# Weight conversion's sign word by GpSimd's rounding addition in place of VectorE's mask, and w_out's row 7 used as a split pair in chunk 0's first half

## The chip, the cores and the metric

The kernel runs on one core of a Trainium2 chip. The metric is device time in microseconds (us), as the median of three runs. The engines are PE (TensorE: matmuls), DVE (VectorE), ACT (ScalarE), POOL (GpSimd) and SP (SyncE, which here only issues DMAs).

## The reference, cut to what matters

```python
B, H, S, Ns, D = (8, 8, 512, 32, 64)      # x: B,H,S,D   state: B,H,Ns,D
scores = scale * np.matmul(x, state.transpose(0, 1, 3, 2))
a = softmax(scores);  xread = np.matmul(a, state)
scores2 = scale * np.matmul(state, x.transpose(0, 1, 3, 2))
a2 = softmax(scores2);  sread = np.matmul(a2, x)
attn_out = np.concatenate([xread, sread], axis=2)
x = attn_out.transpose(0, 2, 1, 3).reshape(B * S, H * D)     # rows: x's and the state's
h = x @ w_in;  g = h - np.tanh(h);  out = g @ w_out           # 512 -> 2048 -> 512
```

`softmax` stands here for the five lines that subtract the maximum, exponentiate, and divide by the sum. `w_in` (512 x 2048) and `w_out` (2048 x 512) arrive as 64-bit floats, so each value is two 32-bit words in memory, and the kernel makes 32-bit floats of them itself.

## The kernel before, in words

The work is cut into chunks: chunk i holds the 512 x-rows of batch i, and a last chunk the rows of the state reads. For a chunk, `hidden(f)` makes one of 16 slices of 128 hidden columns by matmuls into PSUM (`hps`), `finish` makes `t = tanh` on ACT and `g = hps - t` on DVE, and `output(f)` adds g times row f of w_out (128 x 512) into four PSUM banks (`ops`). Since w_in enters only behind the attention, the first chunks multiply the state by w_in once (`mps`, copied to `mr` by ACT) and use that product as the hidden layer's weights.

Most products are made of pairs: a number is split into a high part (ACT's CAST to fp32r) and a rest (DVE's subtraction), both at line 106, and three matmuls (lines 575, 576, 577, or 515, 516, 517) replace one of full precision. In the first half of chunk 0, rows listed in `PLAIN` are not split: one matmul in plain fp32 (line 573) does it, which the profile shows as two records. The attention weights of chunk 1 (`aT`) are ready when DVE has made their low part, and chunk 1's first hidden matmuls wait for them. The program does eight rows of chunk 0, then all of chunk 1, then the rest of chunk 0.

`Weight.load` brings a 128 x 512 block of 64-bit words by SP into one of six buffers (`w10d`, `wo3d` and the like: `w10` is a block of w_in, `wo3` row 3 of w_out). `Weight.steps` makes it 32-bit in four instructions: DVE shifts the high word (line 138), DVE masks the sign bits into a 16-bit field of a helper tile (line 139, `w10r`), ACT writes the low word's rest into the other field (line 140), and DVE adds the two (line 141). The helper tiles, the unsplit rows of w_out (`wor`) and some others share four buffers (tag `c2`). There are 32 such blocks.

Each engine runs its instructions in a fixed order. The start follows the string `SEQ`; behind it a scheduler sets each engine's order when the program is built, from dependences, from `issue_after` gates and from its own estimate of times. `CONV` and `WO` say at which step a block is converted, `SPLITS` at which step a plain row is split for later use.

Of the kernel before, what the change touches and what calls it, by code (L numbers as in the profile page):

```python
# [13 lines left out]
U16 = mybir.dt.uint16  # L14
ALU = mybir.AluOpType
# [15 lines left out]
EARLY_S = 2  # L31
LONE = 1
HALT = 8
PLAIN = (0, 1, 7)
TURN = ((0, 1, 2, 3), (1, 0, 3, 2))


# [1 line left out]
def attention_ffn(ctx: ExitStack, tc: tile.TileContext, xT, xn, bd, bh, sp, sm, sl, win, wout, xout, tout, sout):  # L39
# [10 lines left out]
    nc = tc.nc  # L50
# [57 lines left out]
    class Weight:  # L108
# [17 lines left out]
        def steps(self, dst):  # L126

            if self.src.dtype == F32:
                return [lambda: None] * 3 + [lambda: nc.gpsimd.tensor_copy(dst, self.raw)]
            low, high = self.raw[:, :, 0], self.raw[:, :, 1]  # L130
            u, i = dst.bitcast(U32), dst.bitcast(I32)


            r = pool.tile([P, 512, 2], U16, tag="c2", name=f"{self.name}r", bufs=CSB)
            rest, top = r[:, :, 0], r[:, :, 1]
            return [

                lambda: nc.vector.tensor_scalar(u, high, 3, 0x3FFFFFFF, ALU.logical_shift_left, ALU.bitwise_and),
                lambda: nc.vector.tensor_single_scalar(top, self.raw.bitcast(U16)[:, :, 3], 0xC000, ALU.bitwise_and),
                lambda: nc.scalar.activation(rest, low, AF.Copy, scale=2.0**-29),  # L140
                lambda: nc.vector.tensor_add(i, i, r.rearrange("p f w -> p (f w)").bitcast(I32)),
            ]

        def convert(self, dst):
            return [step() for step in self.steps(dst)][1].ins


    m_first = {}
# [147 lines left out]
    def convert_wout(f, part):  # L296
        if f in PLAIN:
            if f // 2 not in plain:
                plain[f // 2] = big(f"wp{f}", [P, 2, DM], F32)
            return part.convert(plain[f // 2][:, f % 2])  # L300
        w = pool.tile([P, 512], F32, tag="c2", name=f"wor{f}", bufs=CSB)
        made = part.convert(w)
        wo[f] = big(f"wo{f}", [P, 2, DM], F32R)
        low = split(wo[f][:, 0], wo[f][:, 1], w)[1].ins
        return low if f in (2, 3) else made
# [3 lines left out]
    def split_row(f):  # L309
        wo[f] = big(f"wo{f}", [P, 2, DM], F32R)  # L310
        split(wo[f][:, 0], wo[f][:, 1], plain[f // 2][:, f % 2])
# [179 lines left out]
    class Chunk:  # L491
# [31 lines left out]
        def finish(self, f, ps):  # L523
            i, n = self.i, self.n
            t = pool.tile([P, 512], F32, tag="t", name=f"t{i}_{f}", bufs=TB)[:, :n]
            if CL <= i < B:
# [4 lines left out]
                return  # L531
            if i == 0 and f in PLAIN:
                g = self.g[f] = pool.tile([P, 512], F32, tag="g", name=f"g{i}_{f}", bufs=GB)
# [33 lines left out]
        def add(self, f, t):  # L567
            g, o = self.g[f], self.o[t]
            tok = slice(t * P, t * P + P)
            stop = f + 1 in self.begins or f == NFF - 1 or (self.i == B and t == 1 and f == NFF - 3)  # L570
            if self.i == 0 and f in PLAIN:
                w = plain[f // 2][:, f % 2]
# [78 lines left out]

    CONV = [1, 1, 8, 8, 9, 10, 11, 12, 13, 14]
    WO = [0, 2, 3, 4, 5, 6, 9, 10, 11, 12, 13, 14, 15, 16]
    SPLITS = [8,9,10]
    split_it = iter(PLAIN)
    PAIRS = [1, 1, 9, 9, 11, 11, 13, 13, 15, 15]
    rest = w0[1][2:] + w0[2] + w0[3]
# [237 lines left out]
    for st, (i, f) in enumerate(order):  # L895
# [34 lines left out]
            with ExitStack() as gates:  # L930
                for x in tanhs[max(st - 1, 0)]:
                    gates.enter_context(tc.issue_after(x))
                if st in (HALT, HALT + 1):
                    gates.enter_context(tc.issue_after(settled[1]))
                for _ in range(SPLITS.count(st)):
                    split_row(next(split_it))
# [276 lines left out]
```

## Time and profile before

| what | us |
|---|---|
| median of 3 runs | 637.64 |
| lowest, highest run | 637.53, 640.27 |
| span of the profiled execution | 635.4 |
| PE busy in it | 627.7 |
| DVE busy in it | 474.8 |
| ACT busy in it | 380.3 |
| POOL busy in it | 24.0 |

The span goes from the first to the last instruction. The profiled execution's own time is its span and what lies around it; against the median of the runs that is 637.64 - 635.4 = 2.2 us, and a span is turned into a time by adding them. The granted PE clock is 1.000 of full speed over the whole span.

### The profile page before, as it was taken

The numbers are of one execution on the slowest core, as the hardware profiler recorded it, in microseconds if no ns is written. First come the engines' busy times: TensorE is split into PE (matmuls) and PEld (weight loads), VectorE is DVE, ScalarE is ACT, GpSimd is POOL, SyncE is SP. The second block draws the span as 40 slices with busy tenths as digits, with TensorE's granted clock in tenths as the row PEclk, the third lists the DMA queues.
The fourth block names the chain that finished last, engine by engine and source line by source line (L and its number), as shares of the span: only waits on it lengthen the run. The fifth ranks groups of instructions, "written<-read, shape, count | busy, mean of one in ns | idle before, by whom it ended". The sixth has DMA issues, their size and how long they took to land.

```text
span 635.4 us, 9664 instructions
## 1 busy us (share of the span) xinstructions
PE 627.7 (99%) x3490; PEld 489.2 (77%) x3490; DVE 474.8 (75%) x770; ACT 380.3 (60%) x656; POOL 24.0 (4%) x38
## 2 busy tenths in 40 slices
PE   7999999999999999999999999999999999999997
PEld 4456677777777788778888788788888888888996
DVE  5999997686667956999445889989955789754542
ACT  5777777567666757676554675637565554533432
POOL 0000000000000000000000000000000001233200
PEclk9999999999999999999999999999999999999999
DMA  9993866568879856679952644765555537999700
GB/s 319 361 387 132 297 226 183 187 190 254 261 239 294 271 198 219 217 268 346 364 189 87 206 144 141 230 226 163 169 178 181 172 100 239 299 338 329 252 1 33
DMA packets 67439, 141.21 MB, mean 222 GB/s; under 512 B 6976, under 2 KB 28736, under 8 KB 67392
## 3 DMA queue, kind: packets, MB, share of 16 engines
q1 hardware_dynamic: 64544, 131.95, 63.4%
q0 software_dynamic: 2560, 8.39, 4.0%
q8 instruction: 27, 0.44, 0.3%
q10 hardware_dynamic: 288, 0.26, 0.1%
q14 instruction: 20, 0.16, 0.1%
HBM read 96.01 MB, written 44.56 MB: 221 GB/s over the span
## 4 chain that ended last, share of the span: by engine, by line
PE 94%; DVE 3%; ACT 2%; DMA 1%; issue 0%; ACTq 0%
PE X L1048 14%; PE hps L515 10%; PE hps L516 10%; PE hps L517 10%; PE ops L575 10%; PE ops L576 9%; PE ops L577 9%; PE Y0m L1048 5%; PE Y1m L1048 5%; PE mps L242 2%; PE mls L249 2%; PE ops L573 2%; PE rps L461 1%; PE pps L440 1%; PE hps L789 1%; PE mps L187 1%
## 5 line engine op out<-in xcount | busy, mean ns | idle before, releaser
L575 PE MATMUL ops<-wo,g 128*128 128x512 f32 x244 | 96.2, 400 | 0.0
L576 PE MATMUL ops<-wo,g 128*128 128x512 f32 x244 | 95.5, 391 | 0.0
L515 PE MATMUL hps<-aT,m 128*128 128x512 f32 x240 | 94.4, 395 | 0.0
L516 PE MATMUL hps<-aT,m 128*128 128x512 f32 x240 | 93.8, 391 | 0.1
L517 PE MATMUL hps<-aT,m 128*128 128x512 f32 x240 | 93.4, 390 | 0.0
L577 PE MATMUL ops<-wo,g 128*128 128x512 f32 x244 | 88.4, 396 | 0.0
L536 DVE TENSOR_TENSOR t<-hps,t 128x512 f32<-128x512 f32 (+1 forms) x77 | 48.7, 633 | 45.2 <-ACT t L536 44.8
L530 ACT ACTIVATE t<-hps 128x512 f32<-128x512 f32 x64 | 38.4, 599 | 66.3 <-PE hps L517 66.0
L536 ACT ACTIVATE t<-hps 128x512 f32<-128x512 f32 (+1 forms) x77 | 42.5, 552 | 56.7 <-PE hps L517 56.1
L530 DVE TENSOR_TENSOR G<-hps,t 128x512 f32<-128x512 f32 x64 | 43.9, 687 | 28.9 <-ACT t L530 28.7
L106 DVE TENSOR_TENSOR g<-t,g 128x512 fp32r<-128x512 f32 (+1 forms) x77 | 48.5, 632 | 16.1 <-ACT g L106 15.2
L575 PEld LDWEIGHTS ops<-wo,g 128*128 128x128 f32 x244 | 45.6, 188 | 17.4 <-ACT t L536 2.3
L106 ACT CAST g<-t 128x512 fp32r<-128x512 f32 (+1 forms) x77 | 44.3, 576 | 23.2 <-DVE t L536 22.8
L577 PEld LDWEIGHTS ops<-wo,g 128*128 128x128 f32 x244 | 45.5, 188 | 12.6 <-issue 2.5
L515 PEld LDWEIGHTS hps<-aT,m 128*128 128x128 f32 x240 | 45.1, 188 | 12.4 <-issue 2.0
L576 PEld LDWEIGHTS ops<-wo,g 128*128 128x128 f32 x244 | 45.8, 188 | 10.5 <-issue 1.1
L516 PEld LDWEIGHTS hps<-aT,m 128*128 128x128 f32 x240 | 45.1, 188 | 9.9 <-DVE aT L106 0.5
L517 PEld LDWEIGHTS hps<-aT,m 128*128 128x128 f32 x240 | 45.0, 188 | 9.4
L1048 PE MATMUL X<-g0m,W0m 128*128 128x512 f32 x192 | 47.8, 389 | 0.0
L1048 PE MATMUL X<-g1m,W1m 128*128 128x512 f32 x192 | 45.8, 389 | 0.0
L106 ACT CAST g1m<-G 128x1024 fp32r<-128x1024 f32 x28 | 29.2, 1054 | 27.0 <-PE X L1048 9.9
L1086 POOL DMA_DIRECT2D wl<-wod x32 | 23.3, 728 | 574.2 <-DMA wn<-wf 526.6
(275 smaller groups left out, 1134.5 us busy)
## 6 DMA issues: line engine op xcount, KB each, us to landing
mr<-md SPq DMA_DIRECT2D x26, 512.0 KB, 4.3
xT<-in_xT SPq DMA_DIRECT2D x16, 512.0 KB, 6.1
md<-st SPq DMA_DIRECT2D x64, 128.0 KB, 3.1
xn<-in_xn SPq DMA_DIRECT2D x16, 512.0 KB, 5.6
wsd<-ws SPq DMA_DIRECT2D x16, 512.0 KB, 4.7
wod<-wo SPq DMA_DIRECT2D x32, 256.0 KB, 7.3
W0m<-wsd SPq DMA_DIRECT2D x16, 512.0 KB, 3.6
W1m<-wsd SPq DMA_DIRECT2D x16, 512.0 KB, 4.7
```

What stands on the lines that cost most here:

```text
L106: return nc.scalar.copy(hi, src), (sub or nc.vector).tensor_sub(lo, src, hi)
L242: made = nc.tensor.matmul(pss[e], s0[rows, x, 2 * p + e], t[rows, y], start=(n == 0), stop=(n == 2))
L515: nc.tensor.matmul(ps, mhi[k][:, cols], ahi[:, k], start=(k == 0), stop=False)
L516: nc.tensor.matmul(ps, mhi[k][:, cols], alo[:, k], start=False, stop=False)
L517: made = nc.tensor.matmul(ps, mlo[k][:, cols], ahi[:, k], start=False, stop=(k == nk - 1))
L530: main(nc.scalar.activation(t, ps, AF.Tanh), nc.vector.tensor_sub(g, ps, t))
L536: tanhs.append((nc.scalar.activation(t, ps, AF.Tanh).ins, nc.vector.tensor_sub(t, ps, t).ins))
L575: nc.tensor.matmul(o, g[:, 0, tok], w[:, 0], start=(f in self.begins), stop=False)
L576: nc.tensor.matmul(o, g[:, 0, tok], w[:, 1], start=False, stop=False)
L577: return nc.tensor.matmul(o, g[:, 1, tok], w[:, 0], start=False, stop=stop).ins
L1048: made = nc.tensor.matmul(out[t], w[:, e, x, cols], y[:, e], start=first and j == 0 and e == 0 and c == 0, stop=last and j == 3 and e == 1 ...
L1086: nc.gpsimd.dma_start(wo[f][:, :, cols].bitcast(F32), wod[:, f % 2, half, f // 2])
```

## The change

The mask on DVE goes. GpSimd reads the topmost 16 bits of each 64-bit word as a number, adds 1.5 * 2^37 and subtracts it again in 32-bit floats, which rounds to a multiple of 2^14, and writes that into the helper tile's field. The shift on DVE no longer masks. Row 7 leaves `PLAIN`, so it is split when it is converted, its g is split too, and the later split of row 7 goes.

```diff
-PLAIN = (0, 1, 7)
+PLAIN = (0, 1)
+COARSE = 1.5 * 2.0**37
...
-                lambda: nc.vector.tensor_scalar(u, high, 3, 0x3FFFFFFF, ALU.logical_shift_left, ALU.bitwise_and),
-                lambda: nc.vector.tensor_single_scalar(top, self.raw.bitcast(U16)[:, :, 3], 0xC000, ALU.bitwise_and),
+                lambda: nc.vector.tensor_single_scalar(u, high, 3, ALU.logical_shift_left),
+                lambda: nc.gpsimd.tensor_scalar(top, self.raw.bitcast(U16)[:, :, 3], COARSE, COARSE, ALU.add, ALU.subtract),
...
-            return [step() for step in self.steps(dst)][1].ins
+            return [step() for step in self.steps(dst)][0].ins
...
-    SPLITS = [8,9,10]
+    SPLITS = [8,9]
```

The scheduler then sets other orders. In the changed kernel every line behind line 33 has a number one higher. On ACT, in the start, the order before was as follows; `mr` and `at` are what the hidden matmuls of chunk 0's first four slices read, and `w11r` is the helper tile of a block of w_in.

```order
L784 COPY mr_136<-mps_237 64x2x128 x2
L140 ACTIVATE w10r<-w10d 128x512
L784 COPY mr_136<-mps_255 64x2x128 x2
L742 COPY at_275<-aps_267 128x512
L784 COPY mr_187<-mps_237 64x2x128 x2
L784 COPY mr_187<-mps_255 64x2x128 x2
L792 ACTIVATE t_0_287<-hps_0_253 128x512
L792 ACTIVATE t_1_290<-hps_1_251 128x512
L140 ACTIVATE w11r<-w11d 128x512
```

At the same place the changed kernel has this order on ACT.

```order
L785 COPY mr_136<-mps_237 64x2x128 x2
L141 ACTIVATE w10r<-w10d 128x512
L141 ACTIVATE w11r<-w11d 128x512
L785 COPY mr_136<-mps_255 64x2x128 x2
L743 COPY at_275<-aps_267 128x512
L785 COPY mr_187<-mps_237 64x2x128 x2
```

The helper `w11r` has moved ahead of the two copies from `mps_255` and of the copy `at_275`.

Further on, ACT splits row 3 of w_out (`wo_410`). `mps_322` and `mps_323` are the first pair of state-times-w_in products there, `mps_388` and `mps_389` the second pair. Before:

```order
L140 ACTIVATE wo3r<-wo3d 128x512
L207 COPY mr_312<-mps_322 128x512
L106 CAST m_561<-mr_187 128x1024
L207 COPY mr_313<-mps_323 128x512
L106 CAST wo_410<-wor_404 128x512
L140 ACTIVATE wo4r<-wo4d 128x512
L140 ACTIVATE wo5r<-wo5d 128x512
L207 COPY mr_312<-mps_388 128x512
L106 CAST wo_467<-wor_461 128x512
```

The same place on ACT in the changed kernel:

```order
L208 COPY mr_312<-mps_322 128x512
L107 CAST m_563<-mr_187 128x1024
L141 ACTIVATE wo3r<-wo3d 128x512
L208 COPY mr_313<-mps_323 128x512
L208 COPY mr_312<-mps_388 128x512
L208 COPY mr_313<-mps_389 128x512
L107 CAST wo_410<-wor_404 128x512
L537 ACTIVATE t_4_418<-hps_4_415 128x512
```

Row 3's CAST has moved behind both copies of the second pair.

On DVE the subtraction that needs this CAST stood here before, with rows 4 and 5 of w_out behind it.

```order
L141 ISA wor_404<-wor_404,wo3r 128x1024
L106 TENSOR_TENSOR m_561<-mr_187,m_561 128x1024
L106 TENSOR_TENSOR wo_410<-wor_404,wo_410 128x512
L138 TENSOR_SCALAR wor_461<-wo4d 128x512
L139 TENSOR_SCALAR wo4r<-wo4d 128x512
L138 TENSOR_SCALAR wor_502<-wo5d 128x512
```

In the changed kernel the same place on DVE reads as follows.

```order
L142 ISA w_366<-w_366,w13r 128x1024
L142 ISA wor_404<-wor_404,wo3r 128x1024
L107 TENSOR_TENSOR wo_410<-wor_404,wo_410 128x512
L139 TENSOR_SCALAR wor_461<-wo4d 128x512
L139 TENSOR_SCALAR wor_502<-wo5d 128x512
L537 TENSOR_TENSOR t_4_418<-hps_4_415,t_4_418 128x512
```

The masks are gone, and `wo_410` follows at once on the addition of row 3. From here to the first low part of `aT` the changed kernel's DVE list holds what the list before held, without the masks of rows 4 to 7, and with two more subtractions: row 7 of w_out (which stood behind `aT` before) and its g.

## Rows read from the trace of the kernel before

**Rows 1.** The page: span, and busy time, share and instructions of three engines.

```profile
span 635.4 us, 9664 instructions
...
PE 627.7 (99%) x3490; PEld 489.2 (77%) x3490; DVE 474.8 (75%) x770; ACT 380.3 (60%) x656; POOL 24.0 (4%) x38
```

**Rows 2.** Windows: stretch, its length, busy us and instructions, PE clock, DMA share, GB/s.

```profile
37.00:44.40 7.40, 7.40 (x45) 3.95 (x37) 7.40 (x15) 7.02 (x13) 0.00 (x0) 1.00 1.02 386
44.40:55.30 10.90, 10.84 (x43) 7.73 (x42) 10.82 (x22) 5.40 (x11) 0.00 (x0) 1.00 0.40 156
...
62.00:80.00 18.00, 18.00 (x101) 12.54 (x100) 18.00 (x36) 14.45 (x26) 0.00 (x0) 1.00 0.86 295
80.00:120.00 40.00, 40.00 (x212) 29.27 (x211) 33.89 (x58) 28.58 (x51) 0.00 (x0) 1.00 0.64 212
```

**Rows 3.** Waits of PE, 5 to 60 us, its longest: total us, times, longest one.

```profile
PE mps L773 <- DVE w L141: 1.5, 2, 0.9
```

**Rows 4.** The chain in the start: start us, us, what.

```profile
10.54 0.37 DVE w01r L139
...
12.49 0.36 DVE w02r L139
...
13.57 0.63 PE aps L739 x4
```

**Rows 5.** Timeline of ACT, 14 to 24 us: start us, us, instruction.

```profile
17.51 0.78 ACT L140 ACTIVATE w10r<-w10d 128x512 uint16<-128x512 uint32 x1
18.16 0.72 ACT L784 COPY mr<-mps 64x256 f32<-64x256 f32 x2
19.29 0.59 ACT L742 COPY at<-aps 128x512 f32<-128x512 f32 x1 [0.41 <-PE aps L739]
...
22.45 0.78 ACT L140 ACTIVATE w11r<-w11d 128x512 uint16<-128x512 uint32 x1
```

**Rows 6.** Timeline of PE, 16 to 24 us.

```profile
19.09 4.54 PE L789 MATMUL hps<-at,mr 128*128 128x512 f32 x10
```

**Rows 7.** Timeline of SP, 6 to 24 us: the load of w11.

```profile
11.29 0.34 SPq L124 DMA_DIRECT2D w11d<-in_win  x1
```

**Rows 8.** DMA issues, 0 to 30 us: size, us from issue to landing.

```profile
w11d<-in_win SPq DMA_DIRECT2D x1, 512.0 KB, 7.4
```

**Rows 9.** Timeline of ACT, 34 to 41 us.

```profile
37.24 0.59 ACT L207 COPY mr<-mps 128x512 f32<-128x512 f32 x1 [0.64 <-PE mps L187]
37.77 1.22 ACT L106 CAST wo<-wor 128x512 fp32r<-128x512 f32 x2
```

**Rows 10.** Timeline of DVE, 30.8 to 41 us.

```profile
35.08 0.70 DVE L106 TENSOR_TENSOR wo<-wor,wo 128x512 fp32r<-128x512 f32 x1
35.68 0.43 DVE L138 TENSOR_SCALAR wor<-wo4d 128x512 uint32<-128x512 uint32 x1
36.02 0.48 DVE L139 TENSOR_SCALAR wo4r<-wo4d 128x512 uint16<-128x512 uint16 x1
36.37 0.43 DVE L138 TENSOR_SCALAR wor<-wo5d 128x512 uint32<-128x512 uint32 x1
```

**Rows 11.** The chain at the start of chunk 1: start us, us, what.

```profile
54.69 0.58 DVE aT L106
...
55.32 0.50 PE hps L516
...
57.90 3.43 PE ops L573 x8
61.33 0.23 PE hps L515
```

**Rows 12.** Timeline of POOL, 0 to 3 us.

```profile
0.25 0.09 POOL L1198 MEMSET const-float32-0.0<- 128x1 f32 x1 [0.25 <-issue]
...
0.74 0.20 POOL masks.py:197 MEMSET ident<- 128x128 f32 x1 [0.29 <-POOLq L1198]
1.02 0.29 POOL masks.py:199 TENSOR_SCALAR_AFFINE_SELECT ident<-ident 128x128 f32<-128x128 f32 x1
```

## The prediction

> **What bounds the kernel now.** The page comes first: PE is busy for 627.7 of 635.4 us, DVE for 474.8, GpSimd for 24 [rows 1]. That is an average, so the windows come next, for the stretch in which blocks are converted. Between 37 and 44.4 us PE and DVE are both busy without a gap, and from 44.4 to 55.3 us nearly so (10.84 and 10.82 of 10.90) [rows 2]. The waits of PE show the rest: between 5 and 60 us its longest entry is 1.5 us in two waits, for DVE's addition, and that lies in the start [rows 3]. So before the first transposition of the attention weights, which the chain has at 13.57 us, DVE decides [rows 4]; behind it PE is the bound, and DVE runs beside it with hardly a reserve until chunk 1 starts. There the chain crosses over: DVE finishes the low part of aT at 54.69 + 0.58 = 55.27, and PE's first matmul that needs it starts at 55.32 [rows 11]. DVE is still full from 62 to 80 us, and has 6 us to spare from 80 to 120 [rows 2]. A microsecond of DVE ahead of aT is therefore worth nothing or a microsecond, by whether PE or DVE is the later one at 55.3; they are level now.
>
> **What each part costs.** The masks: 32 go from DVE. Starts stand 36.37 - 36.02 = 0.35 us apart behind one [rows 10], so 11 us of DVE go in all. Two stand in the chain of the start, 0.37 and 0.36 [rows 4], and could bring the transposition forward by 0.7 us; the next item takes that back. The shift with one operation for two is costed at nothing: still one pass over 512 elements.
>
> ACT's order in the start. The helper w11r now stands ahead of the copies from mps_255. Its data are issued at 11.29 [rows 7] and land 7.4 us later [rows 8], at 18.69; the DMA queue is full then, so an earlier issue would not land it earlier. Before, the two copies started at 18.16, and w11r was done at leisure at 22.45 [rows 5]. After, ACT stands until 18.69, spends 18.16 - 17.51 = 0.65 on the helper as on w10r [rows 5], and the copies, 0.72 together, end at 20.06. Their reader, the fourth slice of chunk 0's hidden layer, is in the PE row that started at 19.09 [rows 6] and ran ten records without a gap. PE loses 20.06 - 19.09 = 1.0 us, whatever the start gained. Sum so far +1.0.
>
> Row 3's CAST. The second pair of products releases ACT at 37.24, and that is PE's time, not DVE's [rows 9]. ACT now has two copies there and then the CAST of row 3: starts stand 37.77 - 37.24 = 0.53 apart, a CAST lasts 1.22 / 2 = 0.61 [rows 9], so it ends at 37.24 + 2 x 0.53 + 0.61 = 38.91, and DVE's subtraction starts at 38.95 in place of 35.08 [rows 10]. DVE has by then saved its masks, but everything behind the subtraction waits in its queue: rows 4 to 7 of w_out, the g of slices 4 to 7, and the whole softmax that leads to aT. This is 3.87 us, and with the 1.0 that PE is late, 4.87. What DVE saved ahead of it becomes idle time.
>
> From there to aT. The same list took from 35.68 to 55.27, 19.6 us. Four masks leave it (4 x 0.35 = 1.4), and two subtractions join it, row 7's and its g's, at 35.68 - 35.08 = 0.60 each [rows 10], 1.2 together. So aT is late by 4.87 - 0.2 = 4.7 us, and PE, level with DVE before, waits for it: it has no other work queued ahead of those matmuls. Sum +4.7. ACT's added CAST of g is hidden, since ACT is busy for only 5.40 of 10.90 us there [rows 2].
>
> Row 7 on PE. Four plain matmuls, eight records, took 3.43 us [rows 11]; in their place stand 12 of the pair kind at 61.33's 0.23, 2.7 us. They stand behind aT, where PE is the bound: -0.7. The later split of row 7 (one CAST, one subtraction) moves, and was counted. Sum +4.0.
>
> GpSimd beside DVE. No row shows GpSimd at arithmetic on 512 elements. From one column, 0.09, and 128 columns, 0.20 for filling and 0.29 for a selection [rows 12], straight lines give 0.09 + 4 x 0.11 = 0.53 and 0.09 + 4 x 0.20 = 0.89 us for 512; four times the selection would be 1.16. I take 0.7. That alone costs nothing: 32 x 0.7 is 22 us over some 90, and each is done before its addition is due. The open question is whether DVE can work meanwhile. Lower bound: it can, and the sum stays +4.0. Upper bound: each GpSimd instruction stops DVE for its whole length. No row decides. The nearest says that DVE passes 512 elements in 0.34 us with one input (35.68 to 36.02) and in 0.60 with two [rows 10]: reading is what limits it, and a second reader in the same tiles more likely takes from it than not. I take the upper bound. In the queue from row 3's subtraction to aT, where DVE has no idle time, five such instructions fall (wo5r, wo6r, wo7r, w20r, w21r; they wait for buffers that this same queue frees): 5 x 0.7 = 3.5. The sum is 4.0 + 3.5 = +7.5, with 0.53 and 1.16 it is +6.7 and +9.8. Behind aT the 14 that follow take 9.8 us of DVE, in place of 14 x 0.35 = 4.9 for masks; the 6 us to spare up to 120 us [rows 2] cover the difference of 4.9; at 1.16 each it is 11.3, and they would not, by some 5 us.
>
> The rule that bears on this is in the Trainium skill, SBUF — State Buffer, section "Who interferes with whom": GpSimd and DVE share a port pair as a lock, DVE asks for it in its double-rate modes and when it has two inputs in SBUF against a reading GpSimd, and the loser "fully blocks". No row here shows such a pair of instructions. The same skill's GPSIMD Engine Reference, section "Elementwise — side-by-side cycle accounting", gives 769 ns for 512 elements of a tight loop; with that the estimate for the five would be 3.8 instead of 3.5.
>
> The SP queue: loads wait for GpSimd too before they reuse a buffer, but w20 to w23 are not needed before aT. That is costed at nothing, and at most at one GpSimd instruction, 0.9.
>
> **The forecast.** Span 635.4 + 7.5 = 642.9, and with the 2.2 us around it 645.1 us.
>
> **The rivals.**
> 1. GpSimd works beside DVE for nothing, and only the orders count: 637.6 + 4.0 = 641.6. For it: no row shows the engines hindering each other. Against it: the read-limited rates above.
> 2. GpSimd's instruction lasts 0.9 to 1.2 us and hinders: +8.5 at 0.9 (4.0 + 5 x 0.9) to +9.8, and up to 5 more behind aT: 646.1 to 652.4. For it: 16-bit words picked out of 64 and turned into floats and back are unlike a dense fill.
> 3. Not slower: row 3's CAST finds its place without holding DVE. If mps_388 were ready before 33.4 us, 3.87 earlier, the term of 3.87 would vanish, and with the masks ahead of 35 us saved as well, DVE would have aT some 2 us early. Then -0.7 for row 7 and up to -0.7 for the start remain, 636.2. Against it: PE's time at 37.24 is set by PE's own queue, which is full. It decides from the point at which DVE's subtraction of row 3 starts before about 35.5 us.
> 4. The change does not do what it says on DVE, if the shorter shift ran at the two-input rate: 32 x 0.26 = 8.3 us of DVE given back, four of them ahead of aT, 1.0 us more. It adds to another case and is in the range.
>
> **How the numbers follow.** Forecast 0.45 (642.5 to 646), rival 1 0.27 (640 to 642.5), rival 2 0.18, rival 3 0.10. The range reaches from rival 1's lower part to the middle of rival 2: 640 to 651, which leaves out rival 3 and the upper part of rival 2. A run of this kernel tells a difference of about 0.5%, 3.2 us, from none: slower than 637.6 + 3.2 = 640.8 are the forecast, rival 2 and two thirds of rival 1, 0.81; within it the rest of rival 1 and half of rival 3, 0.13; faster 0.06.
>
> **What would show it.** Right: in the start ACT idles before w11r and PE's fourth slice starts near 20.1. DVE idles 3 us ahead of row 3's subtraction, which starts near 40. aT's low part ends near 63.5, and PE waits some 7 us for it. DVE's instructions start late beside each GpSimd one. Without the hindrance aT ends near 60. Wrong: DVE without idle time before that subtraction, or PE without a wait at chunk 1, would take the forecast down; GpSimd instructions near 1.2 us would take it up.

## The result and the profile after

The changed kernel takes 643.33 us (median of 5 runs, 642.93 to 645.81); the kernel before, on the same chip, 637.53 (5 runs). The ratio of the runs is 1.0100, with a 95% interval from 1.0084 to 1.0116 (the two medians alone give 1.0091). The change makes the kernel 1% slower. The two slowest of the five, 645.37 and 645.81, had a mean granted clock of 0.997 and 0.995, the other three 0.999 and 1.000. The profiled spans are 641.4 and 635.4 us, so 6.0 us have to be found.

The page of the changed kernel answers to [rows 1].

```profile
span 641.4 us, 9723 instructions
...
PE 628.2 (98%) x3494; PEld 490.1 (76%) x3494; DVE 473.4 (74%) x739; ACT 381.6 (59%) x657; POOL 99.4 (15%) x70
```

GpSimd has 75 us more than before, and DVE only 1.4 less, although 32 masks are gone. PE has as much to do as before, so it must have been made to wait. The timeline of POOL (start, length, instruction, and in brackets the idle time ahead of it with what ended it) shows how long a sign word takes.

```profile
10.27 2.17 POOL L140 TENSOR_SCALAR w01r<-w01d 128x512 uint16<-128x512 uint16 x1 [1.14 <-DMA w01d<-in_win]
12.32 2.29 POOL L140 TENSOR_SCALAR w02r<-w02d 128x512 uint16<-128x512 uint16 x1
14.55 2.13 POOL L140 TENSOR_SCALAR w03r<-w03d 128x512 uint16<-128x512 uint16 x1
...
41.69 2.26 POOL L140 TENSOR_SCALAR wo5r<-wo5d 128x512 uint16<-128x512 uint16 x1 [2.17 <-DVE wo L107]
48.75 2.13 POOL L140 TENSOR_SCALAR wo6r<-wo6d 128x512 uint16<-128x512 uint16 x1 [4.80 <-DVE wo L107]
```

That is 2.1 to 2.5 us for most of the 32 (the longest 3.59), where a mask cost DVE 0.35. From w01r on they follow each other without a gap in the start, and the chain goes through them (start us, us, what); it answers to [rows 4, 6].

```profile
10.27 2.17 POOL w01r L140
12.44 2.19 POOL w02r L140
14.65 1.12 DVE w L142
15.91 1.13 PE mps L765 x8
...
21.08 4.56 PE hps L790 x10
```

In [rows 4] the steps of w01r and w02r were 0.37 and 0.36 of DVE. PE's row of the fourth slice, which started at 19.09 [rows 6], now starts at 21.08: 2.0 us are lost here. ACT's order is as forecast, but the timeline of ACT shows no idle time ahead of w11r:

```profile
19.04 0.78 ACT L141 ACTIVATE w10r<-w10d 128x512 uint16<-128x512 uint32 x1
19.68 0.76 ACT L141 ACTIVATE w11r<-w11d 128x512 uint16<-128x512 uint32 x1
20.31 0.72 ACT L785 COPY mr<-mps 64x256 f32<-64x256 f32 x2
```

The copies behind w11r end at 20.31 + 0.72 = 21.03, just before PE's row; before, that row stood 0.45 behind the start of the transposition ahead of it, now 0.67. So w11r's new place can have cost 0.2 of the 2.0 us.

The next loss is at row 3 of w_out. On ACT, its CAST stands behind the two copies of the second pair, and these wait for PE:

```profile
39.29 1.07 ACT L208 COPY mr<-mps 128x512 f32<-128x512 f32 x2 [3.07 <-PE mps L188]
40.25 0.63 ACT L107 CAST wo<-wor 128x512 fp32r<-128x512 f32 x1
```

In the timeline of DVE, the subtraction waits for that CAST:

```profile
36.88 0.69 DVE L142 CUSTOM_DVE_ANT_0 wor<-wor,wo3r 128x1024 uint16<-128x1024 uint16 x1
40.91 0.69 DVE L107 TENSOR_TENSOR wo<-wor,wo 128x512 fp32r<-128x512 f32 x1 [3.35 <-ACT wo L107]
41.52 0.42 DVE L139 TENSOR_SCALAR wor<-wo4d 128x512 uint32<-128x512 uint32 x1
41.86 0.91 DVE L139 TENSOR_SCALAR wor<-wo5d 128x512 uint32<-128x512 uint32 x1
...
49.18 0.77 DVE L142 CUSTOM_DVE_ANT_0 wor<-wor,wo5r 128x1024 uint16<-128x1024 uint16 x1
49.87 0.68 DVE L379 TENSOR_TENSOR e<-e,m 128x512 f32<-128x512 f32 x1
50.47 0.68 DVE L537 TENSOR_TENSOR t<-hps,t 128x512 f32<-128x512 f32 x1
...
61.61 1.29 DVE L107 TENSOR_TENSOR aT<-at,aT 128x512 fp32r<-128x512 f32 x2
```

It starts at 40.91 in place of 35.08 [rows 10], 5.83 later. The first low part of aT follows at 61.61, 7.0 later than in the timeline of DVE before:

```profile
54.62 1.46 DVE L106 TENSOR_TENSOR aT<-at,aT 128x512 fp32r<-128x512 f32 x2
```

(The chain of [rows 11] counts the same instruction from 54.69.) DVE needed 20.70 us from the one to the other, where it needed 54.62 - 35.08 = 19.54 before.

What PE lost shows in its timeline, at the four rows that waited between 24 and 63 us:

```profile
39.93 1.98 PE L514 MATMUL hps<-at,mr 128*128 128x512 f32 x4 [0.68 <-ACT mr L208]
...
53.34 0.50 PE L577 MATMUL ops<-wo,g 128*128 128x512 f32 x1 [0.39 <-DVE wo L107]
...
57.42 0.50 PE L577 MATMUL ops<-wo,g 128*128 128x512 f32 x1 [0.88 <-DVE wo L107]
...
61.63 0.73 PE L516 MATMUL hps<-aT,m 128*128 128x512 f32 x2 [2.09 <-ACT aT L107]
```

Before, the longest wait of PE in this stretch was 0.08 us. The four make 4.04 us of idle time, and with the 2.0 of the start 6.0. That this is just the difference of the spans is a coincidence: idle time is counted from the modelled ends of matmuls, and by their starts PE is later. Chunk 1's hidden matmuls start 7.0 later (the row of [rows 11] that began at 55.32 begins at 62.36), and 6.4 later once row 7 is behind them. Row 7 gives back 0.6 of it, and 0.3 more comes back at 239 us, where the kernel before waits once and the changed one does not. The windows of [rows 2], taken in the changed kernel, say the same of both engines (length, then PE, PEld, DVE, ACT and POOL busy):

```profile
37.00:44.40 7.40, 6.72 (x46) 2.50 (x45) 3.96 (x7) 4.90 (x9) 4.74 (x2) 1.00 0.79 271
...
80.00:120.00 40.00, 40.00 (x221) 28.84 (x220) 32.95 (x50) 29.92 (x50) 19.62 (x8) 1.00 0.58 194
```

In the first window DVE is busy for 3.96 us of 7.40, which it filled before: what the masks freed, and more, became idle time ahead of row 3. From 80 us on PE is full again, and GpSimd's 19.6 us beside DVE change nothing.

### The profile page after: what moved, and what is told of

It reads as the page before. It is cut to its first block, busy times and chain, and to the rows that moved or that the text cites. A ratio compares the mean times of both kernels' runs of the same rounds, so it can differ in the third digit from the quotient of the medians.

```text
span 641.4 us, 9723 instructions
## 1 busy us (share of the span) xinstructions
PE 628.2 (98%) x3494; PEld 490.1 (76%) x3494; DVE 473.4 (74%) x739; ACT 381.6 (59%) x657; POOL 99.4 (15%) x70
## 4 chain that ended last, share of the span: by engine, by line
PE 94%; DMA 2%; DVE 2%; POOL 1%; SPq 0%; issue 0%; ACT 0%
PE X L1049 14%; PE hps L516 10%; PE hps L517 10%; PE ops L576 10%; PE hps L518 10%; PE ops L578 9%; PE ops L577 9%; PE Y0m L1049 5%; PE Y1m L1049 5%; PE mps L243 2%; PE mls L250 2%; PE rps L462 1%; DMA w01d<-in_win 1%; PE sps L351 1%; PE hps L790 1%; PE pps L441 1%
## 5 line engine op out<-in xcount | busy, mean ns | idle before, releaser
L577 PE MATMUL ops<-wo,g 128*128 128x512 f32 x248 | 97.1, 392 | 1.3 <-DVE wo L107 1.3
L576 PE MATMUL ops<-wo,g 128*128 128x512 f32 x248 | 96.1, 400 | 0.1
L578 PE MATMUL ops<-wo,g 128*128 128x512 f32 x248 | 90.3, 393 | 0.0
L107 DVE TENSOR_TENSOR g<-t,g 128x512 fp32r<-128x512 f32 (+1 forms) x78 | 49.9, 642 | 16.4 <-ACT g L107 15.2
L576 PEld LDWEIGHTS ops<-wo,g 128*128 128x128 f32 x248 | 46.3, 188 | 18.2 <-issue 3.4
L577 PEld LDWEIGHTS ops<-wo,g 128*128 128x128 f32 x248 | 46.6, 188 | 12.2 <-DVE wo L107 2.1
L578 PEld LDWEIGHTS ops<-wo,g 128*128 128x128 f32 x248 | 46.3, 188 | 11.6 <-issue 2.0
```

Source lines behind the costliest of these rows:

```text
L107: return nc.scalar.copy(hi, src), (sub or nc.vector).tensor_sub(lo, src, hi)
L576: nc.tensor.matmul(o, g[:, 0, tok], w[:, 0], start=(f in self.begins), stop=False)
L577: nc.tensor.matmul(o, g[:, 0, tok], w[:, 1], start=False, stop=False)
L578: return nc.tensor.matmul(o, g[:, 1, tok], w[:, 0], start=False, stop=stop).ins
```

## The experiments

Each kernel is compared with the kernel before in the same set of runs. The median of before was 637.92 us in the set with row 7 alone, GpSimd alone, all but the first six sign words and the last sixteen, and 637.38 in the set with the other four, which ran on another chip.

**Row 7 alone.** The kernel before, with row 7 split and the masks left on DVE.

```diff
-PLAIN = (0, 1, 7)
+PLAIN = (0, 1)
...
-    SPLITS = [8,9,10]
+    SPLITS = [8,9]
```

> Row 7 split, all masks still on VectorE. Theory A, row 7 is PE work and nothing else: 4 plain matmuls (3.43 us) become 12 of the pair kind (2.7 us), so 0.7 us faster, 636.9. Theory B, the two added subtractions (0.60 us each) stand in VectorE's queue ahead of the attention weights of chunk 1, where VectorE and PE are level: +1.2 - 0.7, so 638.0 to 639 and PE's first matmul of chunk 1 starts near 56.5 to 57 us instead of 54.6.

Measured: 639.27 us (638.63 to 641.37), ratio 1.0023 with an interval from 1.0012 to 1.0034. The profile of DVE in this run, at chunk 1, and one of PE's waits behind it (total us, times, longest):

```profile
54.99 0.68 DVE L106 TENSOR_TENSOR g<-t,g 128x512 fp32r<-128x512 f32 x1
55.59 1.29 DVE L392 STREAM_TRANSPOSE at<-e 128x512 f32<-128x512 f32 x2
56.98 1.29 DVE L106 TENSOR_TENSOR aT<-at,aT 128x512 fp32r<-128x512 f32 x2
...
PE ops L575 <- ACT g L106: 0.5, 1, 0.5
```

The low part of aT starts at 56.98, 2.4 later than the 54.62 of before. 1.1 of that came in the first 8 us of this one execution (the DMA of `bdr` landed 0.3 later, and the four matmuls behind it took 1.91 us for 1.09, which the trace does not explain); the other 1.2 to 1.3 are the two subtractions that joined DVE's queue. PE waits 1.1 us there and gets back 0.7 across row 7 (it is 2.4 late ahead of it and 1.7 behind), but at 64.9 it waits 0.5 for a g that ACT casts, and from 75 us on it is 2.6 late. Row 7's split alone makes the kernel slower, since DVE is level with PE at that point.

**GpSimd alone.** The changed kernel with row 7 as before.

```diff
-PLAIN = (0, 1)
+PLAIN = (0, 1, 7)
...
-    SPLITS = [8,9]
+    SPLITS = [8,9,10]
```

> All 32 sign words on GpSimd, row 7 plain. Theory B: start (+2.0) and the wait for row 3's CAST (+3.8) stay, and only row 7's +1.2 - 0.7 goes: 642 to 643.5. Theory A, row 7's extra work ahead of chunk 1 is what costs: 639 or less.

Measured: 643.05 us (642.2 to 643.42), ratio 1.0074 (1.0062 to 1.0086); the span is 640.7. The last matmul of slices 0 to 3 is 2.05 later than before, and the rows of DVE read like those of the changed kernel:

```profile
40.92 0.69 DVE L107 TENSOR_TENSOR wo<-wor,wo 128x512 fp32r<-128x512 f32 x1 [3.31 <-ACT wo L107]
...
60.52 1.29 DVE L107 TENSOR_TENSOR aT<-at,aT 128x512 fp32r<-128x512 f32 x2
```

Nearly all of the loss comes with the sign words, and row 3's wait does too. Two of the five runs had a mean clock of 0.997; the profiled one had 1.000.

**The sign words by place.** Three kernels, all with row 7 as before, put only some blocks' sign words on GpSimd: all but the first six, the first six only, and the last sixteen only. The cut shows the first kernel's condition; the others ask for `in FIRST` and `in LATE`, and the shift on DVE loses its mask for the same blocks.

```diff
+FIRST = ("w00", "w01", "w02", "w03", "wo0", "wo1")
+LATE = [f"w{q}{r}" for q in (2, 3) for r in range(4)] + [f"wo{f}" for f in range(8, 16)]
...
+                lambda: nc.gpsimd.tensor_scalar(top, self.raw.bitcast(U16)[:, :, 3], COARSE, COARSE, ALU.add, ALU.subtract)
+                if self.name not in FIRST
+                else nc.vector.tensor_single_scalar(top, self.raw.bitcast(U16)[:, :, 3], 0xC000, ALU.bitwise_and),
```

All but the first six:

> Sign words of w00 to w03, wo0, wo1 on VectorE, the 26 others on GpSimd, row 7 plain; row 3's CAST then stands ahead of the second pair's copies again on ScalarE. Theory B (places in the queues): the 2.0 us of the start go, and most of the 3.8 us: 638 to 639.5. Rival, GpSimd hinders VectorE for the whole of its 2.1 us instructions ahead of chunk 1 (ten of them): 641 or more.

Measured: 639.46 us (639.09 to 640.71), ratio 1.0027 (1.0017 to 1.0037). The start is 0.1 to 0.3 late, and row 3 waits little, since its CAST stands ahead of the second pair's copies on ACT again. The loss is at aT, whose low part starts at 56.79 in place of 54.62, and there PE waits (the last line, from the waits of PE: total, times, longest):

```profile
35.99 0.62 ACT L108 CAST wo<-wor 128x512 fp32r<-128x512 f32 x1 [2.08 <-DVE wor L147]
...
38.03 1.04 ACT L213 COPY mr<-mps 128x512 f32<-128x512 f32 x2
...
36.64 0.69 DVE L108 TENSOR_TENSOR wo<-wor,wo 128x512 fp32r<-128x512 f32 x1 [0.68 <-ACT wo L108]
...
56.79 1.29 DVE L108 TENSOR_TENSOR aT<-at,aT 128x512 fp32r<-128x512 f32 x2
...
PE hps L521 <- ACT aT L108: 1.8, 1, 1.8
```

Ahead of aT ten masks are gone from DVE, 3.5 us. Eleven GpSimd instructions run beside that stretch, and nine of DVE's instructions there took longer than the median of their form before, by 3.5 us together. So what the masks freed was taken back, and DVE's waits, 1.3 us in all, came on top.

The first six only:

> The reverse of the run with the first six on VectorE: only w00 to w03, wo0 and wo1 by GpSimd, row 7 plain; the helper w11r stands behind the copies on ScalarE, as before. Theory B1: the start is slow because each GpSimd instruction takes 2.1 us and VectorE's additions wait for it, so PE's first product of w02 starts 1.5 us or more later (15.7 or later for 14.17) and the time is 638.5 to 639.7. Rival, the recorded step: ScalarE's wait for w11 ahead of the copies costs PE the time there; with w11r back behind them the start loses nothing, 637 to 637.8.

Measured: 638.9 us (638.33 to 640.1), ratio 1.0024 (1.0014 to 1.0033). Here w11r stands behind the copies on ACT as before (at 24.90 us), and the start is late all the same. DVE's additions wait for GpSimd, and PE's products of w02 start at 15.60 in place of the 14.17 that the timeline of before has, 1.43 later. (The last line shows the windows of this run, with PE's clock as the third number from the end.)

```profile
12.18 1.08 DVE L147 CUSTOM_DVE_ANT_0 w<-w,w01r 128x1024 uint16<-128x1024 uint16 x1 [1.12 <-POOL w01r L143]
...
14.36 1.10 DVE L147 CUSTOM_DVE_ANT_0 w<-w,w02r 128x1024 uint16<-128x1024 uint16 x1
...
15.60 2.05 PE L770 MATMUL mps<-w,sps 128*128 128x128 f32 x8
...
14.50:17.75 3.25, 3.18 (x13) 2.81 (x14) 3.05 (x5) 2.79 (x6) 3.25 (x2) 0.50 1.05 397
```

The last matmul of slices 0 to 3 is 2.45 late, but 1.0 of that came with the clock of this one execution. Behind a wait of PE of 1.95 us, which ended at 13.31, the granted clock stood at 0.50, the lower of its two levels, for 3.4 us, and the eight products took 2.05 us, where they took 1.13 before. The mean clock was 0.997 in this run and in one more of the nine (639.24 and 640.1 us); the other seven, at 1.000, have a median of 638.38, 1.0 us above before.

The last sixteen only:

> Only w20 to w33 and wo8 to wo15 on GpSimd, row 7 plain, so all that lies ahead of chunk 1 is as before. VectorE loses 16 masks (5.6 us) in a stretch in which PE is the bound. Theory B: worth nothing, 637.0 to 638.0, with VectorE's idle time between 62 and 110 us larger. Rival, GpSimd holds VectorE up by its whole length: 16 x (2.1 - 0.35) = 28 us of VectorE, more than its reserve of some 6 us up to 120 us: over 645.

Measured: 637.84 us (636.92 to 638.87), ratio 1.0002 (0.9992 to 1.0011). From 62 to 200 us PE has no wait in this kernel; sixteen masks less, 5.6 us of DVE, are worth nothing, and sixteen sign words on GpSimd cost nothing.

The three ratios add to 0.53%, 3.4 us, where GpSimd alone has 0.74%, 4.7. In none of the three parts does row 3's CAST stand behind the second pair's copies: the order that makes the wait of 3.3 us comes only with all sign words on GpSimd. The 1.3 between the sums (nearer 2 if only runs with a clock of 0.999 or more are taken) is where that order's price may lie; it was not split further.

**Row 3's CAST first.** GpSimd alone, with row 3 converted a step earlier and the copies of the second pair of products kept behind row 3's CAST.

```diff
-    WO = [0, 2, 3, 4, 5, 6, 9, 10, 11, 12, 13, 14, 15, 16]
+    WO = [0, 1, 3, 4, 5, 6, 9, 10, 11, 12, 13, 14, 15, 16]
...
+        with ExitStack() as behind:
+            if (q, k) == (1, 1):
+                behind.enter_context(tc.issue_after(cast3[0]))
```

> All sign words on GpSimd, row 7 plain, and row 3 converted one step earlier, with the second pair's copies told to follow row 3's CAST on ScalarE. The recorded step says that this one place costs 3.87 us: 643.05 - 3.9, 639.2 or up to 640. Rival: the wait is one of several that the new orders hold, and the next one takes its place ahead of the attention weights of chunk 1: 642 to 643.

Measured: 643.19 us (642.74 to 643.89), ratio 1.0092 (1.0078 to 1.0106): not faster than GpSimd alone. The lines are rows of DVE, then the products of w02 on PE in this kernel (L771) and in GpSimd alone (L765), and last this kernel's window from 15 to 18 us:

```profile
38.89 0.69 DVE L107 TENSOR_TENSOR wo<-wor,wo 128x512 fp32r<-128x512 f32 x1 [0.69 <-ACT wo L107]
39.50 0.97 DVE L139 TENSOR_SCALAR wor<-wo4d 128x512 uint32<-128x512 uint32 x1
...
42.73 0.69 DVE L543 TENSOR_TENSOR t<-hps,t 128x512 f32<-128x512 f32 x1 [1.45 <-ACT t L543]
...
15.61 2.04 PE L771 MATMUL mps<-w,sps 128*128 128x128 f32 x8 [0.43 <-DVE w L142]
...
15.96 1.13 PE L765 MATMUL mps<-w,sps 128*128 128x128 f32 x8 [0.53 <-DVE w L142]
...
15.00:18.00 3.00, 2.57 (x10) 2.21 (x10) 2.80 (x5) 2.54 (x6) 3.00 (x2) 0.50 1.04 391
```

The subtraction is 2.0 us earlier, at 38.89, and DVE then stands 1.45 us for the t of a slice, which PE delivers no earlier. The wait at aT is 3.0 us of PE in place of 1.5. But the two kernels do not differ in the CAST alone: the clock was lower in all five runs here (0.995 to 0.997 in the mean). In the profiled one it stood at 0.50 from 14.9 to 18.1 us, behind a wait of PE of 1.86 us, and PE was 0.6 us later than in GpSimd alone when the first pair of state-times-w_in products began (33.07 and 32.48). By 92 us it was 0.1 later. So the new order gave back some 0.5 us, not 3.9, and most of the wait moved to the next places; that it is worth nothing is not shown.

**No sign word.** The kernel before with the masks left out altogether, and ACT writing the whole 32-bit helper word. GpSimd does nothing here, so this is what freeing DVE of the masks is worth at best.

```diff
-                lambda: nc.vector.tensor_single_scalar(top, self.raw.bitcast(U16)[:, :, 3], 0xC000, ALU.bitwise_and),
-                lambda: nc.scalar.activation(rest, low, AF.Copy, scale=2.0**-29),
+                lambda: None,
+                lambda: nc.scalar.activation(r.rearrange("p f w -> p (f w)").bitcast(U32), low, AF.Copy, scale=2.0**-29),
```

> Leaves the sign words out on every engine (ScalarE writes the whole 32-bit helper word, weights lose their sign), row 7 plain: what VectorE's masks cost at most. Theory B: PE is the bound, so 11 us of VectorE are worth only the two masks in the start's chain (0.7 us) and what the queue ahead of chunk 1 gives: 635.5 to 637. Rival, VectorE bounds the stretch up to 80 us: 633 or less.

Measured: 636.15 us (635.89 to 637.37), ratio 0.9985 (0.9976 to 0.9994). The first transposition starts at 12.80, 0.77 before the 13.57 of [rows 4]:

```profile
12.80 0.63 PE L739 MATMUL aps<-ident,e 128*128 128x128 f32 x4
...
30.24 1.09 PE L187 MATMUL mps<-w,sps 64*32 64x512 f32 x16
```

Of the 0.77 only 0.2 is left at the first pair of state-times-w_in products, which start at 30.24 in place of 30.43; the lead is 0.9 at 86 us and 1.2 behind the place at 239 us. So 32 masks less on DVE, 11 us by their starts and 9.8 in the busy time, are worth 1.2 us.

**GpSimd's instruction in other forms.** The kernel before, with an instruction more on GpSimd for each of the last 16 blocks, whose result nothing reads: 256 words 8 bytes apart with two operations (L153), the same with one (L155), 256 words side by side with two (L157), 128 words 8 bytes apart with two (L159).

```diff
+                if form == 0:
+                    nc.gpsimd.tensor_scalar(spare, words[:, :256, 3], COARSE, COARSE, ALU.add, ALU.subtract)
+                elif form == 1:
+                    nc.gpsimd.tensor_single_scalar(spare, words[:, :256, 3], 1.0, ALU.mult)
...
```

> The kernel before, with a GpSimd instruction on the late 16 blocks whose result nobody reads: four forms. Two operations on 256 words 8 bytes apart; one operation on the same; two operations on 256 contiguous words; two operations on 128 words 8 bytes apart. If a fixed cost dominates, all last near 2 us; if the columns do, 256 last 1.1 us and 128 last 0.6; if the 8-byte step does, the contiguous form is below 0.6; if the second operation does, one operation takes half. Time as before, 637 to 638.5.

Measured: a span of 635.4 us, that of before, and a time of 637.28 in its one run. Each form ran four times, and the lengths spread widely (256 words with two operations from 1.09 to 2.56). The shortest of each form, in groups of POOL by shape (in all us, mean ns, then the idle time ahead):

```profile
L157 POOL TENSOR_SCALAR w32x<-w32d 128x256 uint16<-128x256 uint16 x1 | 1.2, 1173 | 2.0 <-DMA w32d<-in_win 2.0
...
L153 POOL TENSOR_SCALAR wo8x<-wo8d 128x256 uint16<-128x256 uint16 x1 | 1.1, 1089 | 0.1
...
L155 POOL TENSOR_SCALAR w31x<-w31d 128x256 uint16<-128x256 uint16 x1 | 0.9, 875 | 0.6 <-DMA w31d<-in_win 0.6
...
L159 POOL TENSOR_SCALAR w23x<-w23d 128x128 uint16<-128x128 uint16 x1 | 0.7, 652 | 0.1
```

With 2.13 for 512 words, the length goes with the words: 0.65, 1.09 and 2.13, about (2.13 - 0.65) / 384 = 3.9 ns for each. The step of 8 bytes costs nothing that shows (1.09 against 1.17), and the second operation 0.2 of 1.09. A cheaper way to write the same sign word on GpSimd is not in these rows.

## Why the prediction was right, and where it was not

The time, 643.33, is 1.8 us under the forecast of 645.1 and inside the 642.5 to 646 that it was given. That the kernel slows, and that DVE waits for row 3's CAST, was right. Two terms were off in opposite directions, the start by 1.0 too little and GpSimd's hold-up by 2.1 too much, so that the total came near by luck in part.

**The start** was taken at +1.0, by w11r ahead of two copies on ACT. It cost 2.0, and by something else: that step failed. w11r's data had landed when ACT came to it, so there was no wait, and its place can have cost 0.2 us at most. The kernel in which w11r stands behind the copies has the late start as well, with PE's products of w02 1.43 us late before its clock plays a part. What costs is the length of GpSimd's instruction: w01r, w02r and their additions are the chain. The forecast said of GpSimd that each instruction is done before its addition is due; that failed in the start. It also had no term for PE's clock. Of the runs of the four kernels with the first six sign words on GpSimd, 11 of 24 had a mean clock of 0.997 or less, of the other kernels tried none of 43, and of the kernel before 2 of 44. The two traces of such runs show the fall in the start, behind a wait of PE of 1.86 and 1.95 us. In the changed kernel and in GpSimd alone, profiled at 1.000, that wait was 1.55 and 1.58.

**GpSimd's length** was taken as 0.7 us, with a bound of 1.16, by rows of a fill and a selection [rows 12]. It is 2.1 to 2.5, three times as much and far outside the bounds. Those rows neither read 16-bit words nor turn them into floats and back; at 128 columns the fill has 0.20, and this instruction 0.65. The Trainium skill's GPSIMD Engine Reference, section "Elementwise — side-by-side cycle accounting", which the prediction cited with 769 ns for 512 elements of a tight loop, is as far off for this instruction.

**GpSimd holding DVE up** was taken as its whole length, five times 0.7, +3.5. Measured, the list from row 3's subtraction to aT took 20.70 us in place of 19.54: with the 0.2 that the list itself lost, the hold-up is 1.4, beside six GpSimd instructions (w22r falls there too). It isn't the length that counts. Beside wo6r's 2.13 us from 48.75 on, DVE's instruction at 49.87, which reads two tiles in SBUF (the on-chip memory of the tiles), keeps its 0.68, and so does the one at 50.47, which reads one there and one in PSUM; only the one at 49.18 has 0.77; beside wo5r the shift at 41.86 has 0.91 in place of 0.42. Added up over all 32, DVE's instructions beside them are longer than the median of their form before by some 7 to 8 us, about 0.23 for each GpSimd instruction, and mostly it is one instruction of DVE that starts 0.1 to 0.6 us behind GpSimd's. The rule of the Trainium skill, SBUF — State Buffer, section "Who interferes with whom", that the loser of the shared port "fully blocks" would have stopped DVE for up to 2.1 us at each of the five, 10.5 in all, if GpSimd had the port first each time; the traces here bear out a small part of that. Rival 1, which took the hold-up as nothing, was as near in time (641.6, 1.7 us too low) but wrong in this point. Rival 2 was right that the instruction is longer than a fill, and wrong that DVE loses its length. (Its middle is 649.3 us, not the 651 at which the range ends.)

**Row 3's CAST** was forecast as a wait of 3.87 us, with the subtraction near 40. It starts at 40.91, after an idle 3.35: 5.83 late, which are the 2.0 of the start and 3.83. The size is right where it stands. What the prediction did not see is that it isn't an independent price: with the CAST moved ahead, the subtraction came 2.0 us earlier, and the time didn't fall. Part of that is the lower clock of that kernel; by PE's starts some 0.5 us was won.

**Row 7** was forecast as two subtractions ahead of aT, 1.2, against -0.7 on PE. (12 x 0.23 is 2.76 and not 2.7; the term stays -0.7.) The split alone costs 0.23%, 1.4 us, which is more than the two terms leave together (0.5). PE did win the 0.7 across row 7, but lost 0.5 at once at the next wait for a g, so that little of the term is left: it was taken as kept to the end. The sign is as reckoned; of the size, the run's interval reaches down to 0.8 us.

**PE's wait at chunk 1** was forecast at some 7 us and is 2.1. aT is late by 7.0 in place of the forecast 8.2, but PE had lost 4 us by then: 2.0 in the start, and 1.95 at three waits, 0.68 of it for ACT's copy of the second pair and 1.27 for low parts of w_out that the late DVE queue made. The end is as late as with one wait.

**The masks and the shift.** That the freed DVE time is worth next to nothing was right: 1.2 us at best without any sign word, and 0.1 us with an interval around nothing for the late half on GpSimd. The shift with one operation has 0.42 as before, so rival 4 fell. Rival 3 asked for row 3's subtraction before 35.5 us; in no run with sign words on GpSimd ahead of it was it there. Its start, a gain of 0.7, exists only when nothing replaces the masks, and then 0.2 of it is left at 30 us.

What stays open: what row 3's place on ACT costs alone at an undisturbed clock, in the 1.3 to 2 us by which GpSimd alone costs more than its three parts; and why the clock falls in some executions and not in others.

No version tried here with sign words on GpSimd is faster than the kernel before.

## What to carry to other kernels

Moving work from a busy engine to an idle one pays only where the busy one ends a wait: ask for the kernel with that work left out, which here would have shown 1.2 us to be had for 11 us freed. The other engine's length counts wherever its result is in a chain, as 2.1 us for 0.35 was in the start. Where two engines are level, as DVE and PE are here at chunk 1, an added instruction ahead of their meeting costs about its length, 1.2 us for row 7's two, and the 0.7 saved behind was mostly lost again at the next wait. And a kernel whose engine waits longer in the start should be compared by its clock too: the row 3 experiment differed from its partner in both.

## What the hardware showed that was not expected

- GpSimd's two-operation instruction from 16-bit words to 16-bit words took 0.65 us for 128 words in each partition, 1.09 for 256 and 2.1 for 512, six times DVE's mask.
- Beside it DVE mostly kept its speed, with one input and with two, and lost about 0.23 us for each GpSimd instruction on average.
- GpSimd's own length varies beside a busy DVE: the same form of 256 words had 1.17 us once and 3.33 another time, and the sign words of the changed kernel went up to 3.59. Beside the 3.33, DVE's seven instructions all kept their length; beside the 1.17, one took 0.88 in place of 0.68. That DVE holds GpSimd up fits this, and was not tested.
- Behind waits of PE of 1.86 and 1.95 us in the start, the granted clock stood at 0.50 for about 3 us in two traces, and eight matmuls took 2.04 and 2.05 us in place of 1.13.
